# A hand-written issue order replaced by another: the backward chain of a recurrent attention layer

## The chip, the cores and the metric

The kernel runs on one core of one Trainium2 chip. The metric is the device time in microseconds (us) of one execution. The five engines are TensorE (PE, matrix products), VectorE (DVE), ScalarE (ACT), GpSimd (POOL) and SyncE (SP). Each runs its own instructions in the order in which they were issued, and waits on semaphores for the others. Here SP only issues DMAs; POOL issues DMAs too, and copies tiles.

## The reference

The reference is a forward pass and its gradients. `A` is attention with a recurrent memory over 64 segments, `B` a dense layer with a squared ReLU; both work on the same normed input.

```python
for s in range(n_seg):                       # 64 segments of 32 rows, 8 memory rows in front
    h = jnp.concatenate([mem, xs], axis=1)
    q, k, v = (jnp.einsum('btd,dhe->bhte', h, W) for W in (Wq, Wk, Wv))
    scores = jnp.where(mask, jnp.einsum('bhqe,bhke->bhqk', q, k) * scale, -1e9)
    o = jnp.einsum('bhqk,bhke->bhqe', softmax(scores), v)
    o = jnp.einsum('bhte,hed->btd', o, Wo)
    mem = o[:, :M, :]                        # the next segment's memory
    outs.append(o[:, M:, :])
...
_out, _vjp = jax.vjp(_f, A_x, A_mem0, A_Wq, A_Wk, A_Wv, A_Wo, B_w1, B_b1, B_w2, B_b2)
_grads = _vjp(grad_out)
```

The model width is 512; there are 32 heads of 128. The memory makes the segments a chain: forward from segment 0 to 63, and the gradients backward from 63 to 0. All outputs are bfloat16.

## The kernel before

The kernel has these stages: the norm and the dense layer; the forward chain; a pass over the "left" rows (the memory rows of four segments at a time, taken together); the backward chain, which is the one changed; and the products for the weight gradients.

**The backward chain.** One segment is a *step* (`bwd`, L1307), and four steps are a *block*. Steps run from segment 63 down, 64 in 16 blocks; "step 0" to "step 3" below are the places in a block in the order of time. A step on PE is, by the names in the order:

- `o0mm`, `o1mm`: two projections of the incoming gradient by Wo (L391), 16 matmuls each. `o0ev`, `o1ev` evict them (ACT); `o0fl`, `o1fl` transpose them, `o0te`, `o1te` (DVE) evict those. They read tile `GT`, in which the step before put its memory gradient (`Ha`, `Hb`); that is the chain.
- `vp0`, `vp1`: products for the gradient of v, with tiles `PD` and `PGD` (L1379, L1381); `vea`, `veb`, `vla`, `vlb` evict them (ACT).
- `s0`, `s1`: scores' gradients (L436), then four DVE operations each, `d10` to `d40` and `d11` to `d41` (L538 to L548), which give `gS`, and a transpose on DVE, `tu0`, `tu1` (L449).
- `kp0`, `kp1` and `qp0`, `qp1`: 32 short products each (L589) for the gradients of k and q. `kp` needs `gS` and `qN`; `qp` needs the transposed `gS`, `kN` and `kLs`. Evictions: `kea`, `keb`, `kla`, `klb`, `qea`, `qeb`, with a 0 or 1.
- `vg`, `kg`, `qg`, 0 and 1: six long products with the weights (L459), 16 matmuls of 512 columns each, all summed in one bank; the last one's second half goes to another bank.
- `ra`, `rb`: the sum's eviction; `ta`, `tb`: four transposes (L494); `Ha`, `Hb`: sums over head groups into the next step's `GT`; `xa`, `xb`: the other rows.

Pairs of products share PSUM tiles: `vp`, `kp0`+`qp0` and `kp1`+`qp1` take the same two tiles in turn, so each waits for the evictions of the one before.

**Left work**, once a block, for the block before (`left`, L1208): twelve products of eight matmuls, `L.G0` to `L.I3` (L1247), their sums `L.ra0` to `L.ra3`, `L.ta`, `L.tb`, `L.xt`; DMA transposes `L.vtr`, `L.ktr`, `L.qtr` into tile `gNat` (one buffer) and their stores `L.vst`, `L.kst`, `L.qst`; the stores of tiles `G4` (gv, gk, gq; one buffer for four steps) in halves, `L.vo0` to `L.ko1` (512 KB each); and `L.gs`, `L.gst`, `L.sl`, `L.sx`, `L.lq`, `L.gl`, `L.ldt`, `L.ldv`, `L.ldk`, which load the next block's tiles or store this one's.

**Loads of a step.** A load that is played at one step fetches for the next step (L1473). On POOL's queue: `ldp` (tile P, two buffers), `ldq` (qN), `ldn` (kN), with the copies `pb` (P into PD, four) and `vc` (two) between them on the same engine. On SP's queue: `ldk` (kLs, four DMAs of 16 KB) and `vtr` (a DMA transpose into `vl`). All but P have one buffer, so each waits until its tile's last reader is done.

**The order.** All of this is issued from a written list, `B_ORDER` (L1148): four strings, one after the other for each block. `play` (L623) reads them; each plus sign shifts an entry to a step (or, behind "L.", a block) one later. The list alone sets the order on every engine and in every queue: a waiting instruction holds up all that stands behind it on its engine. Which engine evicts what is set apart (`ENGS`), and stays.

Of the kernel before, what the change touches and what calls it, by code (L numbers as in the profile page):

```python
# [26 lines left out]
def kernel(  # L27
# [35 lines left out]
    L = M + SEG  # L63
# [119 lines left out]
    with sb("p1b", 2) as p1b, sb("p1", 1) as p1:  # L183
# [66 lines left out]
        for rb in range(NRB):  # L250
# [45 lines left out]
            xb = p1b.tile([P, RCB, D], BF16, name="xb", tag="xb", bufs=1)  # L296
# [322 lines left out]
    def on_engines(act, vec):  # L619

        return dict([(n, acp) for n in act.split()] + [(n, vcp) for n in vec.split()])
# [365 lines left out]
    with sb("la", 2) as la, sb("ls", 2) as ls, sb("lo", 1) as lo_, sb("wg", 2) as wg, psum("lpp", 1) as lpp, psum("lr", 4) as lr:  # L987
# [158 lines left out]


    B_ORDER = (  # L1148
# [6 lines left out]
        "tb++++ Ha++++ Hb++++",  # L1155
# [5 lines left out]
        "rb++++ ta++++ L.vtr+ ldp+++++ Ha++++ tb++++ Hb++++",  # L1161
# [5 lines left out]
        "tb++++ ldp+++++ Hb++++",  # L1167
        "o0mm++++ o1mm++++ L.ldt++ o0ev++++ ldq+++ ldn+++ vc+++ L.ra3+ xb+++ o1ev++++ xa+++ vtr++++ o0fl++++ "
# [4 lines left out]
        "L.I0++ ra++++ rb++++ ta++++ kla1++++ tb++++ L.H0++ Ha++++ Hb++++ L.ldk++")  # L1173
    ENGS = on_engines(
        "L.ra0 kea0 keb0 keb1 kla0 kla1 o0ev o1ev qea0 qea1 qeb0 ra vea veb vla vlb",
        "kea1 klb0 klb1 o0te o1te qeb1")
# [497 lines left out]
```

## Time and profile before

| | |
|---|---|
| median of three runs | 2915.46 us (2913.0 to 2922.69) |
| profiled execution | 2925.15 us, of which its span 2923.3 |
| PE busy | 2721.1 us, 93% of the span |
| backward chain | 1400.1 to 2345.8 us of the span, 945.7 us |
| DMA engines' busy share in it | 0.74 |
| mean granted clock of PE in it | 0.96 |

The profile is of one execution. Times in it are from the start of the span. "Busy" is the time in which an engine had an instruction under way; matmuls overlap. A line like "L459 PE MATMUL" names the source line, which can be that of a helper. The waits view names who ended an engine's idle time; the chain view follows the last instruction back to what released it at each step. "SPq" is a DMA being issued by SP; its time there is the issue, and the data land later.

### The profile page before, as it was taken

What the parts mean: (1) busy time and instruction counts of PE and PEld (TensorE: products, weight loads), DVE (VectorE), ACT (ScalarE), POOL (GpSimd) and SP (SyncE); (2) the same over time, 40 slices, a digit from 0 to 9 for tenths busy, and PEclk for the clock granted to TensorE, in tenths of its full rate; (3) what the DMA queues carried; (4) which work ended last, traced back from release to release, by engine and by line L of the source; (5) the groups of instructions that cost most, each with busy time, mean ns of one, the idle gap of its engine ahead of it and who ended that gap; (6) DMA issues with size and microseconds to landing.
All of it is one profiled execution on the core that took longest, in us unless ns stands there. A gap on an engine that the chain in (4) does not pass through costs nothing.

```text
span 2923.3 us, 116288 instructions
## 1 busy us (share of the span) xinstructions
PE 2721.1 (93%) x51700; PEld 1476.2 (50%) x51700; DVE 1297.6 (44%) x3790; ACT 1030.6 (35%) x2362; POOL 655.3 (22%) x1262
## 2 busy tenths in 40 slices
PE   7997899999999888889899999998999899999999
PEld 3453455555555555547445545554555444444444
DVE  5452466666666565444445544554455401100000
ACT  2332354444544444433333433433343301111111
POOL 0000100000000001122434343343333324332221
PEclk9998899999999999899899999999999999999999
DMA  9639367677776676999577777777777799999993
GB/s 249 214 101 292 94 166 191 178 193 184 181 196 171 166 170 167 230 260 259 145 181 176 175 197 202 177 183 201 189 172 184 215 280 226 222 211 234 205 206 79
DMA packets 796536, 564.17 MB, mean 193 GB/s; under 512 B 584593, under 2 KB 687138, under 8 KB 792706
## 3 DMA queue, kind: packets, MB, share of 16 engines
q1 hardware_dynamic: 753922, 424.58, 63.3%
q0 software_dynamic: 42112, 132.16, 14.4%
q8 instruction: 405, 6.64, 1.0%
q14 instruction: 97, 0.79, 0.1%
HBM read 191.51 MB, written 234.37 MB: 146 GB/s over the span
## 4 chain that ended last, share of the span: by engine, by line
PE 77%; DMA 11%; DVE 5%; SPq 3%; issue 3%; ACT 1%; POOL 0%; ACTq 0%; DVEq 0%; POOLq 0%
PE ps_gw L1635 17%; PE ps_proj L391 15%; PE ps_gR L459 11%; PE ps_R L459 5%; PE ps_L L349 3%; PE b_pp L589 3%; PE ps_tr L164 3%; PE ps_RL L1247 3%; DMA b_kLs<-S_NL 3%; PE ps_w L1102 2%; PE ps_sc L436 2%; PE f_pp L589 2%; PE b_T L494 1%; PE f_T L494 1%; PE ps_w L1097 1%
## 5 line engine op out<-in xcount | busy, mean ns | idle before, releaser
L1635 PE MATMUL ps_gw<-gn,HNc 128*128 128x512 bf16 x1920 | 416.8, 379 | 0.0
L1635 PEld LDWEIGHTS <-HNc 128*128 128x128 bf16 x1920 | 187.8, 98 | 223.6
L373 ACT CAST f_N<-ps_proj 128x512 bf16<-128x512 f32 x320 | 183.8, 580 | 202.5 <-PE ps_proj L391 200.9
L1568 ACT CAST wt<-ps_gw 128x512 bf16<-128x512 f32 x128 | 74.1, 587 | 450.6 <-PE ps_gw L1635 402.2
L391 PEld LDWEIGHTS <-X 128*32 128x32 bf16 x6144 | 154.3, 96 | 149.8 <-DVE X L503 21.4
L1551 DVE TENSOR_TENSOR gx<-ps_rows,gb 128x512 f32<-128x512 f32 x16 | 11.1, 692 | 426.6 <-PE ps_rows L1549 426.6
L891 POOL COPY kM<-f_kT 128x256 bf16<-128x256 bf16 x64 | 25.6, 400 | 739.9 <-DVE f_kT L376 565.9
L1635 PE MATMUL ps_gw<-GOc,gn 128*128 128x512 bf16 x640 | 141.6, 384 | 10.9 <-ACT wt L1568 9.4
L459 PE MATMUL ps_gR<-Wv,gv 128*32 128x512 bf16 x2048 | 145.9, 407 | 1.2 <-issue 1.2
L391 PE MATMUL ps_proj<-Wq,X 128*32 128x512 bf16 x2048 | 136.1, 382 | 7.2 <-DVE X L962 4.5
L459 PE MATMUL ps_gR<-Wk,gk 128*32 128x512 bf16 (+1 forms) x2048 | 141.1, 390 | 1.4 <-ACT gk L373 0.7
L373 ACT CAST gk<-b_pp 128x256 bf16<-128x256 f32 x192 | 70.7, 379 | 179.7 <-PE b_pp L589 116.0
L459 PE MATMUL ps_R<-Wo,OT 128*32 128x256 bf16 x4096 | 132.9, 286 | 1.1 <-DVE OT L376 1.1
L391 PE MATMUL ps_proj<-Wk,X 128*32 128x512 bf16 x2048 | 133.1, 384 | 0.7
L373 ACT CAST gON<-ps_proj 128x512 bf16<-128x512 f32 x128 | 74.9, 585 | 156.9 <-PE ps_proj L391 156.9
L391 PE MATMUL ps_proj<-Wv,X 128*32 128x512 bf16 x2048 | 129.9, 378 | 0.0
L391 PE MATMUL ps_proj<-Wo,GT 128*32 128x512 bf16 x2048 | 124.2, 384 | 4.2 <-DVE GT L1292 3.5
L1569 POOL DMA_DIRECT2D out_dram<-wt x120 | 64.8, 542 | 258.3 <-ACT wt L1568 243.5
L459 PE MATMUL ps_gR<-Wq,gq 128*32 128x512 bf16 (+1 forms) x2048 | 118.5, 343 | 0.9 <-issue 0.9
L1328 POOL COPY PD<-b_P 32x320 bf16<-32x320 bf16 x256 | 114.7, 448 | 8.0
L459 PEld LDWEIGHTS <-OT 128*32 128x32 bf16 x4096 | 108.1, 101 | 9.3 <-DVE OT L376 1.3
L1323 POOL DMA_DIRECT2D b_P<-S_A x63 | 33.8, 537 | 336.9 <-issue 103.5
(281 smaller groups left out, 5352.6 us busy)
## 6 DMA issues: line engine op xcount, KB each, us to landing
S_A<-f_N SPq DMA_DIRECT2D x64, 512.0 KB
out_dram<-wt POOLq DMA_DIRECT2D x134, 128.0 KB, 5.1
S_A<-f_N SPq DMA_DIRECT2D x64, 256.0 KB
S_GB<-gv SPq DMA_DIRECT2D x32, 512.0 KB
S_GB<-gq SPq DMA_DIRECT2D x32, 512.0 KB
S_GB<-gk SPq DMA_DIRECT2D x32, 512.0 KB
b_kN<-S_A POOLq DMA_DIRECT2D x63, 256.0 KB, 4.5
b_qN<-S_A POOLq DMA_DIRECT2D x63, 256.0 KB, 3.9
```

What stands on the lines that cost most here:

```text
L164: nc.tensor.transpose(ps_ap, in_ap, ident[base:base + k, base:base + k])
L349: nc.tensor.matmul(ps[:], lhsT=x(dc), rhs=Wqkv[t][:, dc, c0:c0 + 512], start=(dc == 0), stop=(dc == DC - 1))
L373: nc.scalar.copy(out, in_)
L391: nc.tensor.matmul(o, lhsT=hT[:, dc, :], rhs=x, start=(dc == 0), stop=(dc == DC - 1), tile_position=(0, 32 * g))
L436: nc.tensor.matmul(sc3[32 * g:32 * g + 32, k, c:c + n], lhsT=qT[:, 4 * h + k, g, :], rhs=kT[:, 4 * h + k, g, :], start=(mask is None), sto ...
L459: nc.tensor.matmul(R[32 * g:32 * g + 32, 0:(cs.stop - cs.start) * P].rearrange("p (a b) -> p a b", b=P), lhsT=XT(k, g), rhs=x[:, cs, :], s ...
L589: nc.tensor.matmul(o, lhsT=N_[32 * g:32 * g + m, kk * P:(kk + 1) * P], rhs=X(kk)[32 * g:32 * g + m], start=(i == 0), stop=(i == len(jobs) ...
L1247: nc.tensor.matmul(ps["R", i][32 * g:32 * g + 32, :].rearrange("p (a b) -> p a b", b=P), lhsT=B_[n][:, k, g, :], rhs=W(g * KH + k), start= ...
L1328: nc.gpsimd.tensor_copy(PD[32 * g:32 * g + 32, g], C["P"][32 * g:32 * g + 32, :, 0:L])
L1568: nc.scalar.copy(wt[:], ps[:])
L1569: eng(dst, wt[:])
L1635: nc.tensor.matmul(ps[:], lhsT=l(rc), rhs=r(rc), start=(n == 0), stop=(n == RC_ALL - 1))
```

## The change

`B_ORDER` is replaced by another list of the same 292 entries. Nothing else is changed: the same operations on the same engines, with the same tiles and buffers. The short products of a step, its evictions, loads and copies, and the left work stand at other places. The new strings are cut at other points than the old ones (a step begins inside a string), so the plus signs differ too.

```diff
     B_ORDER = (
-        "o0mm++++ pb+++ o1mm++++ L.vo1+ L.qst o0ev++++ L.vo0+ xa+++ L.xt L.qo0+ o1ev++++ o0fl++++ xb+++ L.ra0+ "
-        "vp0++++ o0te++++ L.G2+ vea++++ s0++++ d10++++ o1fl++++ d20++++ ldp++++ d30++++ ldq+++ vla++++ o1te++++ "
-        "vp1++++ ldn+++ ldp+++++ L.I1+ L.G1+ vlb++++ d40++++ veb++++ L.ko0+ s1++++ d11++++ L.ko1+ ldk+++ kp0++++ "
-        "vg1++++ tu0++++ L.qo1+ keb0++++ d21++++ qp0++++ kla0++++ vg0++++ kea0++++ d31++++ qeb0++++ d41++++ "
-        "kg0++++ klb0++++ vtr++++ tu1++++ qp1++++ ldn++++ L.sx+ qeb1++++ qea0++++ qg0++++ qea1++++ kp1++++ "
-        "qg1++++ keb1++++ kea1++++ kg1++++ vc++++ klb1++++ kla1++++ ra++++ pb++++ rb++++ ldq++++ L.H2+ ta++++ "
-        "tb++++ Ha++++ Hb++++",
-        "o0mm++++ o0ev++++ o1mm++++ o1ev++++ xb+++ o0fl++++ vp0++++ xa+++ o0te++++ vla++++ s0++++ o1fl++++ "
...
+        "Hb++ o0mm+++ o1mm+++ L.H3 L.lq+ xb++ o0ev+++ o0fl+++ o1ev+++ xa++ o0te+++ ldn++ vp0+++ vea+++ o1fl+++ "
+        "o1te+++ s0+++ vp1+++ s1+++ d10+++ d20+++ ldq++ d30+++ vg0+++ vlb+++ L.gl+ d40+++ kp0+++ vla+++ veb+++ tu0+++ "
+        "d11+++ qp0+++ keb0+++ d21+++ pb+++ d31+++ kla0+++ d41+++ qea0+++ vg1+++ klb0+++ kea0+++ L.vo1+ L.ra3 kg0+++ "
+        "L.ldv+ kp1+++ klb1+++ qeb0+++ tu1+++ L.qo0+ qg0+++ qp1+++ kea1+++ kla1+++ keb1+++ L.ldk+ kg1+++ qea1+++ "
+        "qeb1+++ qg1+++ ra+++ L.G0+ rb+++ ta+++ tb+++ Ha+++ Hb+++ o0mm++++ o1mm++++ L.ta L.ktr+",
+        "L.vo0+ xb++ o0ev+++ o0fl+++ vc++ o1ev+++ vp0+++ vea+++ L.qo1+ xa++ o0te+++ o1fl+++ L.ko0+ ldp+++ s0+++ "
+        "o1te+++ vtr+++ ldn++ vla+++ L.kst+ d10+++ ldk++ vp1+++ s1+++ d20+++ d30+++ d40+++ L.I0+ L.vtr+ vlb+++ L.H0+ "
+        "L.ko1+ ldq++ tu0+++ L.tb kp0+++ qp0+++ L.xt veb+++ keb0+++ kea0+++ L.gs+ ldq+++ d11+++ pb+++ d21+++ L.sx+ "
+        "qeb0+++ klb0+++ kla0+++ vg1+++ vg0+++ d31+++ qea0+++ kg0+++ d41+++ tu1+++ vc+++ qg0+++ qp1+++ kp1+++ L.vst+ "
+        "qea1+++ L.ra0+ qeb1+++ klb1+++ kea1+++ keb1+++ kla1+++ qg1+++ kg1+++ ra+++ ldn+++",
...
```

Read out for a block in the middle (the block of left work is the one before, `L.lq`, `L.gl`, `L.ldt`, `L.ldv`, `L.ldk` load for the next block; "now" marks a load for the step in which it is played, the others are for the next one), PE's products stand so:

```
step 0 before: o0mm o1mm o0fl vp0 G2 s0 o1fl vp1 I1 G1 s1 kp0 vg1 qp0 vg0 kg0 qp1 qg0 kp1 qg1 kg1 H2 ta tb
step 0 after:  o0mm o1mm L.ta o0fl vp0 o1fl s0 vp1 s1 I0 H0 L.tb kp0 qp0 vg1 vg0 kg0 qg0 qp1 kp1 qg1 kg1 I1 ta tb
step 1 before: o0mm o1mm o0fl vp0 s0 o1fl vp1 H1 s1 vg0 kp0 qp0 vg1 qg0 kp1 kg0 qp1 I2 kg1 qg1 G3 ta tb
step 1 after:  o0mm o1mm G1 o0fl vp0 o1fl s0 vp1 s1 vg0 kp0 qp0 vg1 qg0 kg0 kp1 qp1 kg1 qg1 H1 ta tb
step 2 before: o0mm o1mm o0fl vp0 s0 o1fl vp1 vg0 s1 kp0 vg1 qp0 I3 kg0 kp1 qp1 qg0 kg1 qg1 H3 ta tb
step 2 after:  o0mm o1mm G2 o0fl vp0 o1fl s0 vp1 s1 vg0 H2 kp0 qp0 vg1 kg0 I2 qg0 kp1 qp1 G3 kg1 qg1 I3 ta tb
step 3 before: o0mm o1mm o0fl vp0 o1fl s0 vp1 s1 vg0 kp0 L.tb qp0 vg1 kg0 kp1 G0 qp1 L.ta qg0 kg1 qg1 I0 ta tb H0
step 3 after:  o0mm o1mm H3 o0fl vp0 o1fl s0 vp1 s1 vg0 kp0 qp0 vg1 kg0 kp1 qg0 qp1 kg1 qg1 G0 ta tb
```

And the queues of SP and POOL:

```
SP before    step 0: vo1 qst vo0 qo0 ko0 ko1 ldk(now) qo1 vtr sx       step 1: ldk(now) ktr vtr vtr(step 3) kst ldk L.vtr
             step 2: sl vst gs gl gst                                  step 3: ldt vtr ldk(now) qtr lq
SP after     step 0: ktr vo0 qo1 ko0 vtr kst ldk(now) L.vtr ko1 gs sx vst ldk   step 1: qtr vtr gst
             step 2: sl ldk(now) vtr vtr(step 0) ldk ldt qst           step 3: lq gl vo1 qo0
POOL before  step 0: pb(now) ldp ldq(now) ldn(now) ldp(step 2) ldn vc pb ldq    step 1: ldp(step 3)
             step 2: ldq(now) vc(now) pb(now) ldn(now) ldp(step 0)     step 3: ldq(now) ldn(now) vc(now) pb(now) vc ldv L.ldk
POOL after   step 0: vc(now) ldp ldn(now) ldq(now) ldq pb vc ldn       step 1: ldp ldp(step 3) pb ldn vc
             step 2: ldq(now) ldp(step 0) pb vc                        step 3: ldn(now) ldq(now) pb ldv L.ldk
```

More of the change, by code (lines that the diff above doesn't have):

```diff
@@ L1148 @@
     B_ORDER = (
[6 rows of a table removed]
-        "tb++++ Ha++++ Hb++++",
[5 rows of a table removed]
-        "rb++++ ta++++ L.vtr+ ldp+++++ Ha++++ tb++++ Hb++++",
[5 rows of a table removed]
-        "tb++++ ldp+++++ Hb++++",
-        "o0mm++++ o1mm++++ L.ldt++ o0ev++++ ldq+++ ldn+++ vc+++ L.ra3+ xb+++ o1ev++++ xa+++ vtr++++ o0fl++++ "
[4 rows of a table removed]
-        "L.I0++ ra++++ rb++++ ta++++ kla1++++ tb++++ L.H0++ Ha++++ Hb++++ L.ldk++")
[4 rows of a table added]
+        "qeb1+++ qg1+++ ra+++ L.G0+ rb+++ ta+++ tb+++ Ha+++ Hb+++ o0mm++++ o1mm++++ L.ta L.ktr+",
[5 rows of a table added]
+        "rb++ L.I1+ ta++ ldk++ tb++ Ha++ Hb++ o0mm+++ L.qtr+ ldp+++ o1mm+++ o0ev+++ L.G1+ o0fl+++ o1ev+++ xb++ vp0+++ "
[3 rows of a table added]
+        "qea1+++ vc+++ klb1+++ kla1+++ qg1+++ L.H1+ ra+++ ta+++ rb+++ tb+++ Ha+++ Hb+++",
[4 rows of a table added]
+        "vc+++ L.I3+ vtr++++ kla1+++ ra+++ L.ra2+ rb+++ ldk+++ L.ldt++ L.qst+ ta+++ Ha+++ tb+++")
     ENGS = on_engines(
```

20 rows, old and new, of the table B_ORDER are left out of this document.

## The prediction

> **What bounds the kernel now.** I read the page first, then the stretches of the changed stage, then who ended TensorE's waits there, then one block on SP's queue and in the chain of waits.
>
> ```profile
> span 2923.3 us, 116288 instructions
> PE 2721.1 (93%) x51700; PEld 1476.2 (50%) x51700; DVE 1297.6 (44%) x3790; ACT 1030.6 (35%) x2362; POOL 655.3 (22%) x1262
> ```
>
> TensorE (PE) bounds the kernel, but its busy share hides short waits. The backward chain is the stretch 1400.1 to 2345.8 us. One block of it (four steps; step 3 is 1795.0, then step 0 of the next block and its steps 1 and 2) follows under it:
>
> ```profile
> core 0: us, PE busy (x) PEld busy (x) DVE busy (x) ACT busy (x) POOL busy (x), PEclk, DMA share, GB/s
> 1400.10:2345.80 945.70, 881.58 (x22878) 478.43 (x22879) 464.92 (x1454) 360.44 (x980) 365.62 (x708) 0.96 0.74 187
> 1795.00:1810.20 15.20, 13.82 (x365) 7.49 (x368) 7.50 (x24) 5.49 (x15) 8.64 (x17) 1.00 0.81 215
> 1810.20:1827.10 16.90, 15.64 (x372) 8.11 (x368) 6.93 (x24) 6.05 (x16) 4.32 (x9) 0.90 1.02 247
> 1827.10:1840.20 13.10, 12.93 (x357) 7.27 (x356) 7.92 (x23) 5.34 (x15) 5.21 (x11) 1.00 0.54 111
> 1840.20:1853.30 13.10, 12.68 (x350) 6.87 (x348) 6.33 (x21) 5.53 (x15) 4.60 (x9) 1.00 0.78 166
> ```
>
> All steps do nearly the same work, yet steps 3 and 0 take 15.2 and 16.9 us against 13.1. From the timeline's first `o0mm` matmuls the means are 16.6, 13.3, 13.0 and 15.5 us (steps 0 to 3), 58.4 a block. In step 0 the DMA engines are full (1.02) and the granted clock is 0.90. Who makes PE wait, and what SP issues just then:
>
> ```profile
> PE b_pp L589 <- DMA b_kLs<-S_NL: 12.8, 16, 3.2
> PE b_pp L589 <- DVE gS L548: 6.5, 9, 0.9
> PE b_pp L589 <- DMA b_qN<-S_A: 3.0, 4, 1.6
> ```
>
> ```profile
> 1802.79 0.37 SPq L1234 DMA_DIRECT2D S_GB<-gv  x1
> 1803.21 0.42 SPq L1279 DMA_DIRECT2D S_GL<-gNat  x1
> 1803.68 1.15 SPq L1234 DMA_DIRECT2D S_GB<-gv  x1
> 1804.92 0.57 SPq L1234 DMA_DIRECT2D S_GB<-gq  x1
> 1805.54 4.38 SPq L1234 DMA_DIRECT2D S_GB<-gk  x2
> 1809.96 4.78 SPq L608 DMA_DIRECT2D b_kLs<-S_NL  x4
> ```
>
> ```profile
> 1809.96 8.25 DMA b_kLs<-S_NL
> 1818.21 0.05 issue
> 1818.26 0.18 PE b_pp L589
> ```
>
> The last two fences are the mechanism. `qp0` of step 0 needs `kLs`, four loads of 16 KB on SP's queue. They are issued behind five 512 KB stores of G4, land at 1818.2, 15.5 us after the first store was issued and 23.3 us after step 3 began, and are on the chain. Over 14 blocks the product after `qp0` starts 24.3 us after step 3 began, and step 0 ends 7.6 us later: 31.9 for steps 3 and 0 together, 26.35 for steps 1 and 2.
>
> **The change, part by part.** No instruction is added or removed; both orders hold the same 4,672 entries. What moves:
>
> *Inside a step.* (a) `o1fl` now stands ahead of `s0`, so `vp0` and `o1fl` cover `o0te`. In steps 1 and 2 `s0` waits 0.19 us today; saved twice. (b) `qp0` follows `kp0` directly. `kp0` starts some 0.14 us after `d40` ends and its slot is 0.3; `tu0` takes 0.43 and 0.1 to be seen: 0.2 of waiting, in steps 1 and 3. Step 0 and step 2 have left products ahead of `kp0`, which hide it. `kp0` itself waits 0.2 to 0.25 for `d40` in steps 1 and 3 (0.18 today in step 2). (c) In step 0 only `kp1` (0.29) lies between `qp1` and `qg1`, in step 1 only `qp1` (0.30) between `kp1` and `kg1`; an eviction takes 0.37 and 0.25 to start and be seen: 0.33 lost each time. (d) left products: steps 1 and 2 get seven instead of five, at 0.45 to 0.5 each; step 3 gives three away, its rest lies ahead of a DMA wait. Laid end to end from slots of the trace (first matmul to first matmul of the next, unthrottled: two projections 1.84, six gathers 5.6, the small products 2.9, two sums 0.75; 11.15 a step), step 1 is 11.15 + 1.0 + 0.25 + 0.25 + 0.33 + 0.1 = 13.1, step 2 is 11.15 + 2.4 + 0.2 = 13.75. Checked on today's step 2: 11.15 + 1.0 + 0.9 of waits = 13.05, seen 13.03. Steps 1 and 2 together: 26.85, 0.5 more than now. Between none of their waits (25.9) and twice them (27.9) I take the laid-out value.
>
> *Queues.* This is the larger part. SP's order around step 0 becomes `vo1`, `qo0` (now in step 3), `ktr`, `vo0`, `qo1`, `ko0`, `vtr`, `kst`, and only then step 0's `ldk`. Ahead of `ldk` there were `vo1`, `qst`, `vo0`, `qo0`, `ko0`, `ko1`. So five stores of 512 KB stand ahead of it as before, but also two DMA transposes, and a store (`kst`) that waits for one of them to land; everything behind `kst` in SP's queue (`ldk`, `L.vtr`, `ko1`, `gs`, `sx`, `vst`) waits with it, and PE waits for `ldk`.
>
> Prices from the trace's packet list in this stage, as time of all 16 DMA engines: 142,743 packets of 256 bytes hold them 258 us, nine transposes a block in 16 blocks: 1.79 us each. 33,805 packets of 1 KB, 101 us: a gq or gk half (512) 1.53. 4,096 of 4 KB on SP's queue, 42 us: a gv half (128) 1.3. 12,288 of 2 KB, 78 us: an S_GL store (128) 0.81. 13,971 of 4 KB on POOL's queue, 183 us: a 256 KB load (64) 0.84. Work ahead of `ldk` on SP's queue: before 2 x 1.3 + 0.81 + 3 x 1.53 = 8.0; after 2 x 1.3 + 3 x 1.53 + 2 x 1.79 + 0.81 = 11.6. POOL's loads beside it (PGD, gOL, GL, qNL, P, qN, kN) are the same 4.65.
>
> When does it start? `vo1` waits for `veb` of step 3: `vp1` ends at 3.93 (1.84 of projections, H3 0.44, the flips, `vp0` and `s0`), then vlb, vla and veb follow on ScalarE at 3.8, 4.0 and 4.2, veb takes 0.59, so `vo1` goes out 4.95 us into step 3, against 7.8 in the block shown. `qo0` waits for `qeb0` (`qp0` ends at 6.1, five evictions 0.3 apart: 7.4), `ktr` for `kla1` and `klb1` after `kp1` (8.8), `qo1` for `qea1`, `qeb1` after `qp1` (10.6); `vtr` for POOL's `vc` at 11.05 (`pb` from 4.0, five `ldv` issues to 8.5, two `ldk` to 9.6, two copies of 1.45). DMA engines busy from 6.5, 0.6 idle between, 16.25 of work: 23.3. The other way: 4.95 + 15.5 as seen + 3.6 more = 24.0. I take 23.6 for `kLs`; bounds 21 (the half us idle gone and a fifth of the packets faster) and 25.5.
>
> PE's own order would want it sooner: step 3 is 11.15 + 1.0 (H3, G0) + 0.25 + 0.25 + 0.1 = 12.75, and `qp0` stands 5.65 into step 0 (1.84 + sums of the block before 0.37 + 0.43, flips, `vp`, `s` 1.75, I0 and H0 0.95, `kp0` 0.3): 18.4 in all. So PE waits about 5 us there, and the 0.2 waits of step 3 and the slow `d40` (next) vanish in it. After it come 0.3 + 7.7 (`vg1`, `vg0`, `kg0`, `qg0`, `qp1`, `kp1`, `qg1`, `kg1`, I1, `ta`, `tb` = 0.98 + 0.88 + 0.88 + 0.98 + 0.3 + 0.29 + 0.33 + 0.87 + 0.87 + 0.95 + 0.37) and the clock. The trace's clock record has 13 half-speed stretches in the stage after its first 20 us, 51 us together, all in steps 0 and 3: 25.6 lost, 1.6 a block. One 3.41 us stretch a block costs 1.7; between 0.5 and 3.4 I take that, as the wait is longer than most now.
>
> The row on the clock: step 0 above has 0.90, though its longest PE gap is 0.86 us. The Trainium skill (TensorE: Matmul & The Clock Gate, "HAM oscillation — how this bites in real kernels") puts the limit at idle gaps of about 3.4 us. By that rule a wait under 3.4, `kLs` before 21.8, would cost no clock, and the sum there would be 25 us lower than by the row; this trace speaks against it.
>
> *DVE and POOL.* `pb` (four copies of 0.45) now lies at 4.0 to 5.95 of step 3, over `d40`. Today `vc` lies there, and `gS` L548 takes 0.97 instead of 0.32 in half the blocks. Nothing or 0.65, hidden behind `kLs` either way. POOL's other loads go out 1 to 2 us earlier against step 0 and cost nothing while `kLs` is last.
>
> *Sum.* Steps 3 and 0: 23.6 + 0.3 + 7.7 + 1.7 = 33.3 against 31.9, at 15 passages: +21. Steps 1 and 2: +0.5 x 16 = +8. Together +29. The profiled execution was 2925.15 (span 2923.3 and 1.85 around it), 9.7 above the median of the runs; the sum would make it 2954, and on the median 2915.5 + 29 = 2944.
>
> **Rivals.**
> A, faster: the ring is not backed up, because the stores start 2.9 us earlier and are spread. `kLs` lands at 19, PE hardly waits, half the clock loss goes: 19 + 0.3 + 7.7 + 0.5 = 27.5, 4.4 less at 15 passages, -66 + 8: 2858. It decides from `kLs` before 21.7 (31.9 - 0.5 - 9.7). For it: the stage's DMA share is 0.74, and steps 1 and 2 have room. Against: 1.02 in step 0, and `kLs` issues that take 4.78 us for four. Chance 0.22.
> B, slower still: `ko1` now waits behind `L.vtr`, which waits for `kst` to land; it lands near 29, while `keb1` of step 0, which overwrites what it reads, wants 28.4 to 30. ACT waits up to 1.1, PE with it, and a second half-clock stretch follows (1.7): 2.8 x 15 = 42 on the forecast: 2986. Chance 0.14.
> C, no change: the two waits balance, or the order does not do what its words say because PE's queue order hardly matters behind the same DMA bytes: 2915. Chance 0.12.
>
> **The numbers.** The forecast has 0.52. Slower by over 0.3% (9 us, about what a measurement of this kernel tells from none) are it and B: 0.66; faster A: 0.22; the same 0.12. The low end, 2892, is `kLs` at 20.1; the high end, 2987, takes in B and `kLs` at 25.5 (+1.9 x 15 = 28).
>
> **What would show it.** Right: in step 0 a PE gap of 4 to 6 us inside `qp0`, ended by `kLs`; SP's `kst` issued after a wait for `gNat`; steps 1 and 2 at 13.1 and 13.8; a half-clock stretch in most step 0s; `s0` without a wait. Wrong: steps 3 and 0 together under 31, or `kLs` landing before `qp0` is due; or the time lost in steps 1 and 2, in waits between `kp1` and the gathers, which I have priced by rows of other neighbours.

## The result and the profile after

The changed kernel takes 3034.64 us (median of four runs, 3026.39 to 3043.02) against 2918.08 of the kernel before beside it: a ratio of 1.041 [1.037, 1.045], 117 us slower. The forecast was 2944, +29. The direction was right; the size was not: 3035 lies above the high end of the range, 2987. The profiled execution took 3026.43, with a span of 3024.6.

The page of the kernel after first:

```profile
span 3024.6 us, 116331 instructions
PE 2732.1 (90%) x51700; PEld 1486.3 (49%) x51700; DVE 1300.3 (43%) x3790; ACT 1023.8 (34%) x2362; POOL 656.4 (22%) x1262
```

PE has 11 us more of busy time in a span that is 101 us longer: most of the time went into waits, not into work. The stretches of the backward chain, and of one block in it (step 3, then step 0 of the next block, its steps 1 and 2):

```profile
core 0: us, PE busy (x) PEld busy (x) DVE busy (x) ACT busy (x) POOL busy (x), PEclk, DMA share, GB/s
1386.24:2448.83 1062.59, 901.99 (x22878) 494.51 (x22879) 468.59 (x1455) 354.13 (x980) 366.96 (x709) 0.94 0.67 167
1832.04:1846.10 14.06, 12.86 (x350) 6.89 (x350) 7.31 (x22) 5.34 (x15) 8.25 (x16) 1.00 0.92 243
1846.10:1867.12 21.02, 15.70 (x361) 8.89 (x360) 7.39 (x25) 5.74 (x16) 3.15 (x6) 0.84 0.84 226
1867.12:1881.28 14.16, 12.73 (x349) 7.00 (x348) 6.72 (x21) 5.34 (x15) 6.52 (x14) 1.00 0.67 118
1881.28:1896.63 15.35, 13.78 (x373) 7.66 (x372) 7.92 (x23) 5.54 (x15) 4.73 (x9) 1.00 0.31 67
```

The stage is 1062.6 us instead of 945.7, 117 more, which is all of the loss (the execution profiled before had spent 14 us more ahead of the stage, so the spans differ by less). Step 0 takes 21.0 us, of which PE is busy 15.7, at a granted clock of 0.84. The DMA engines are less busy over all of step 0 than before (0.84 against 1.02), as the step is longer; up to the point for which PE waits they are nearly full, as shown below. Who ends PE's waits in the stage, and ACT's for a store:

```profile
PE b_pp L589 <- DMA b_kLs<-S_NL: 49.4, 20, 4.6
ACT gv L373 <- DMA S_GB<-gv: 39.1, 13, 4.8
PE b_pp L589 <- DVE gk L376: 18.6, 32, 0.6
PE b_pp L589 <- ACT b_gkL L373: 14.9, 16, 0.9
PE b_pp L589 <- ACT b_gvL L373: 14.3, 10, 2.8
```

Two families are seen. `kLs` makes PE wait four times as long as before, and `vea` (ACT writes gv) now waits for `vo0` to land, and `kp0` of step 0 with it (the line of `b_gvL`: `kp0` takes the PSUM tile that `vea` and `vla` evict). The lines of `gk` and `b_gkL` came to under 1 us each before: they are now 48 waits inside the steps for evictions, 0.58 and 0.93 us each in the mean. SP's queue in the block shown:

```profile
1837.02 0.34 SPq L1229 DMA_DIRECT2D S_GB<-gv  x1
1839.55 0.54 SPq L1229 DMA_DIRECT2D S_GB<-gq  x1
1842.76 1.27 SPq L1265 DMA_TRANSPOSE gNat<-b_gkL  x1
1844.08 0.57 SPq L1229 DMA_DIRECT2D S_GB<-gv  x1
1844.76 0.56 SPq L1229 DMA_DIRECT2D S_GB<-gq  x1
1845.37 1.68 SPq L1229 DMA_DIRECT2D S_GB<-gk  x1
1847.14 5.04 SPq L1331 DMA_TRANSPOSE b_vl<-S_A  x1
1852.27 0.53 SPq L1274 DMA_DIRECT2D S_GL<-gNat  x1
1852.89 2.30 SPq L608 DMA_DIRECT2D b_kLs<-S_NL  x4
```

The order is the one that the prediction read from the list: `vo1`, `qo0`, `ktr`, `vo0`, `qo1`, `ko0`, `vtr`, `kst`, `ldk`. From step 3's start (1832.04) `vo1` goes out at 4.98 and `qo0` at 7.51 (4.95 and 7.4 were forecast), but `ktr` at 10.7 instead of 8.8 (11.4 in the mean), and the issue of `vtr` alone holds SP for 5.04 us. `kst` goes out 0.09 us after it, here and in each of the 15 passages from a step 3 to a step 0: it does not wait for the tile that `ktr` fills, as the prediction had it. The chain of waits runs through it to PE:

```profile
1852.89 0.32 SPq L608
1853.21 0.06 issue
1853.27 3.62 DMA b_kLs<-S_NL
1856.89 0.05 issue
1856.94 0.77 PE b_pp L589 x19
```

`kLs` lands at 1856.89, 24.85 us after step 3 began; the product behind `qp0` starts at 25.6 in this block and at 26.5 in the mean. From the issue of `vo1` to this landing, in the block shown of the kernel before and then in this one (columns as above):

```profile
1802.79:1818.21 15.42, 13.36 (x338) 7.18 (x326) 6.76 (x24) 4.99 (x13) 5.24 (x12) 1.00 0.97 332
1837.02:1856.89 19.87, 13.94 (x385) 7.72 (x381) 9.21 (x30) 5.25 (x15) 7.37 (x14) 0.93 0.94 253
```

The DMA engines are nearly full in both, 0.97 and 0.94. That is 15.0 us of transfers before and 18.7 after: `kLs` is late because its place in the queue has more transfers ahead of it, not because the engines stand idle.

### The profile page after: what moved, and what is told of

The parts are those of the page before. It is cut to its first block, busy times and chain, and to the rows that moved or that the text cites. A ratio compares the mean times of both kernels' runs of the same rounds, so it can differ in the third digit from the quotient of the medians.

```text
span 3024.6 us, 116331 instructions
## 1 busy us (share of the span) xinstructions
PE 2732.1 (90%) x51700; PEld 1486.3 (49%) x51700; DVE 1300.3 (43%) x3790; ACT 1023.8 (34%) x2362; POOL 656.4 (22%) x1262
## 3 DMA queue, kind: packets, MB, share of 16 engines
q0 software_dynamic: 42112, 132.16, 14.6%
## 4 chain that ended last, share of the span: by engine, by line
PE 74%; DMA 9%; SPq 5%; DVE 5%; ACT 4%; issue 3%; POOL 0%; ACTq 0%; DVEq 0%; POOLq 0%
PE ps_gw L1630 16%; PE ps_proj L391 14%; PE ps_gR L459 11%; PE ps_R L459 4%; PE b_pp L589 3%; PE ps_L L349 3%; PE ps_tr L164 3%; SPq L1331 2%; DMA b_kLs<-S_NL 2%; PE ps_RL L1242 2%; PE ps_w L1102 2%; PE ps_sc L436 2%; PE f_pp L589 1%; PE f_T L494 1%; ACT gk L373 1%
## 5 line engine op out<-in xcount | busy, mean ns | idle before, releaser
L391 PEld LDWEIGHTS <-X 128*32 128x32 bf16 x6144 | 152.3, 96 | 149.6 <-DVE X L503 21.6
L891 POOL COPY kM<-f_kT 128x256 bf16<-128x256 bf16 x64 | 25.6, 400 | 733.9 <-DVE f_kT L376 559.9
L459 PE MATMUL ps_gR<-Wk,gk 128*32 128x512 bf16 (+1 forms) x2048 | 157.3, 389 | 20.9 <-DVE gk L376 8.9
L459 PE MATMUL ps_gR<-Wv,gv 128*32 128x512 bf16 x2048 | 156.7, 438 | 1.7 <-issue 1.7
L459 PE MATMUL ps_gR<-Wq,gq 128*32 128x512 bf16 (+1 forms) x2048 | 128.3, 348 | 10.9 <-ACT gq L373 8.7
L459 PEld LDWEIGHTS <-gk 128*32 128x32 bf16 x2304 | 66.5, 101 | 93.4 <-ACT gk L373 34.5
L459 PEld LDWEIGHTS <-gq 128*32 128x32 bf16 x2816 | 86.8, 99 | 52.0 <-ACT gq L373 19.3
```

Of the source, the lines that this page charges most:

```text
L391: nc.tensor.matmul(o, lhsT=hT[:, dc, :], rhs=x, start=(dc == 0), stop=(dc == DC - 1), tile_position=(0, 32 * g))
L459: nc.tensor.matmul(R[32 * g:32 * g + 32, 0:(cs.stop - cs.start) * P].rearrange("p (a b) -> p a b", b=P), lhsT=XT(k, g), rhs=x[:, cs, :], s ...
```

## The experiments

All are edits of the list alone. Every kernel does all of the work. Step lengths are means over the blocks, from the first `o0mm` matmul of a step to that of the next. The "clock" column is the time that a block loses to half-speed stretches (half of their length).

| kernel | ratio to before | steps 3+0 | steps 1+2 | clock |
|---|---|---|---|---|
| before | 1 | 32.1 | 26.4 | 2.0 |
| after | 1.041 [1.037, 1.045] | 36.2 | 29.5 | 4.0 |
| e1_ldk_first | 1.035 [1.031, 1.038] | 35.5 | 29.3 | 2.6 |
| e2_evictions | 1.025 [1.022, 1.028] | 35.6 | 27.0 | 4.2 |
| e3_both | 1.021 [1.018, 1.024] | 35.9 | 26.5 | 3.6 |
| e7_stores_first | 1.007 [1.004, 1.009] | 31.7 | 27.9 | 2.2 |
| e7b_stores_without_evictions | 1.018 [1.014, 1.021] | 31.9 | 30.4 | 1.8 |
| e9_sx_early | 1.003 [1.001, 1.006] | 32.4 | 27.1 | 2.3 |
| e11_after_repaired | 1.007 [1.004, 1.010] | 32.4 | 27.1 | 2.3 |
| e4_before_transposes_first | 1.024 [1.019, 1.028] | 36.8 | 26.0 | 4.2 |
| e5_before_kea1_first | 1.001 [0.998, 1.003] | 32.3 | 26.4 | 1.6 |
| e6_before_ldk | 1.002 [1.000, 1.005] | 32.6 | 26.2 | 2.2 |
| e8_before_stores_early | 1.012 [1.009, 1.016] | 32.4 | 26.2 | 1.6 |
| e10_before_stores_early_2 | 1.012 [1.009, 1.015] | 33.6 | 25.9 | 2.4 |

**e1_ldk_first: is the place of `ldk` the loss?**

```diff
 step 3, SP's queue
-  vo1 qo0 | ktr vo0 qo1 ko0 vtr kst ldk(step 0) L.vtr ko1
+  vo1 qo0 ldk(step 0) | ktr vo0 qo1 ko0 vtr kst L.vtr ko1
```

> The changed kernel with one entry moved: the load of kLs for step 0 is played in step 3, directly behind qp1 (its buffer's last reader), so in SP's queue it stands ahead of ktr, vo0, qo1, ko0, vtr and kst instead of behind them. PE's order is the same. Queue theory (kLs is late because of what stands ahead of it on SP's queue, and the half clock in step 0 follows from that wait): the 2.5 us inside qp0 of step 0 go, and about half of the 3.4 us that the clock costs there; 15 passages, some 65 us less, near 2968. Rival (the same bytes must pass whatever the order, so another transfer takes its place, first of all vo0, whose landing vea waits for, or qN): under 20 us less, above 3010. Rival (the short waits between products carry all of the loss): no change, 3034.

Measured: 3020.1 us, 0.6% of before less than after (the two intervals touch), as the first rival had it: under 20 us. The wait for `kLs` is gone, and others stand in its place, over the whole stage:

```profile
ACT gk L373 <- DMA S_GB<-gk: 64.2, 30, 4.2
ACT gv L373 <- DMA S_GB<-gv: 42.6, 12, 6.5
DVE gk L376 <- DMA S_GB<-gk: 41.2, 15, 4.5
PE b_pp L589 <- ACT b_gvL L373: 28.1, 14, 4.6
```

`kea` and `keb` of step 0 write tiles that `ko0` and `ko1` still read, `vea` one that `vo0` reads; G4 has one buffer. PE's wait behind `vea` doubles, from 14.3 to 28.1 us. `kLs` was only the last of several transfers that are late together. So the forecast's single term (`kLs` late) was too simple, and its rival B (`ko1` late) was waiting behind it, to show as soon as the first is removed. What fell is the clock's loss, from 4.0 to 2.6 us a block.

**e2_evictions: the waits inside the steps.**

```diff
 order of products and evictions in the list (excerpt)
-step 1: kg0 kp1 kea1 qp1 keb1          step 2: keb0 kea0 kla0 qp0 ... qg0 kp1 tu1 kea1 qp1
+step 1: kp1 kea1 keb1 kg0 qp1          step 2: qp0 keb0 kea0 kla0 ... kp1 tu1 kea1 keb1 qg0 qp1
-step 3: qg0 qp1 kea1 kla1 keb1         step 0: qg0 qp1 kp1 qea1 qeb1
+step 3: kea1 kla1 keb1 qg0 qp1         step 0: qp1 qea1 qeb1 qg0 kp1
```

> The changed kernel with the evictions and the second short products at other places of a step, the queues as they are: in step 3 kea1, kla1, keb1 ahead of qg0 and qp1; in step 0 qp1, qea1, qeb1 ahead of qg0; in step 1 kp1, kea1, keb1 ahead of kg0; in step 2 qp0 ahead of keb0, kea0, kla0, and kp1, tu1, kea1, keb1 ahead of qg0. Tile theory (an eviction listed between two products that share a PSUM tile makes the second product wait for it, and one listed behind the second product waits for that): the slots kp1 to qp1 (0.65 in steps 1 and 2), kp0 to qp0 of step 2 (0.91), qp1 to kg1 of step 3 (0.8), kp1 to qg1 of step 0 (0.7) fall to 0.1 to 0.3; 1.1 us in step 1 and 1.4 in step 2 for 16 blocks, and about 1.5 in steps 3 and 0 together, since kla1 lets ktr out 1.9 us earlier: 55 to 65 us less, near 2975. Rival (kLs alone): steps 1 and 2 gain at most the 10 us of my old sum, above 3020.

Measured: 2989.4 us, 1.6% of before less than after. Step 2 falls from 15.31 to 13.44, step 1 from 14.15 to 13.51. PE's waits in the stage, for the same evictions as above:

```profile
PE b_pp L589 <- DMA b_kLs<-S_NL: 59.9, 22, 5.3
PE b_pp L589 <- ACT b_gkL L373: 5.0, 13, 0.4
```

The wait for ACT's `gkL` is a third of what it was, DVE's `gk` has left the list, and `kLs` has grown by 10 us. **e3_both** has both edits.

> Both edits in the changed kernel: the load of kLs for step 0 behind qp1 of step 3, and the evictions and short products moved. If the two causes are all and independent: 3034 less 65 and less 55, near 2915, what the kernel before takes. If they share a cause (a full ring whatever the order): near 2960. Below 2900 only if the clock loss in step 0 goes entirely.

Measured: 2981.1 us. Steps 1 and 2 are at 26.5, as before the change; steps 3 and 0 still take 35.9, since the stores stand as in e1: in the stage ACT waits 52.9 us to write gv until `S_GB<-gv` has landed, and 70.1 to write gk. What is left is in SP's queue.

**e7_stores_first and e7b: the stores of G4 ahead of the transposes.**

```diff
 SP's queue (e7: e3 and this; e7b: e1 and this)
-  vo1 qo0 ldk(step 0) | ktr vo0 qo1 ko0 vtr kst L.vtr ko1 gs sx vst
+  vo1 vo0 qo0 ldk(step 0) qo1 ko0 ko1 | ktr vtr kst L.vtr gs sx vst
```

> The changed order with step 0's ldk behind qp1 of step 3 and the short products moved ahead of their long ones (as in e3_both), and now also all six stores of G4 ahead of the DMA transposes: vo1 and vo0 directly behind veb of step 3, qo1, ko0 and ko1 behind qeb1; then ktr, vtr, kst. Theory (step 0 waits for whichever of kLs and the G4 stores stands last behind ktr, vtr and kst): the waits ahead of kp0 (1.97 us a block, vea waits for vo0) and ahead of kg1 (1.96, keb1 and kea1 wait for ko1) go down to some 0.2 each, and about 2 of the 3.28 us of clock with them: 5.5 x 15 = 83 us off 2981, so 2890 to 2905, under the kernel before. Rival (the DMA engines are full in step 0, so that any order only moves the wait): the wait shows up behind another load or store, and the time stays at 2960 to 2985.

> The stores and ldk as in e7, with the short products where the changed kernel has them. Theory: step 0 is repaired as in e7, steps 1 and 2 stay as slow as after the change (13.9 and 15.3 us): 2940 to 2955, some 45 us above e7. Rival (full DMA engines): 3005 to 3020, as e1_ldk_first.

Measured: 2940.5 and 2977.6 us. The theory's mechanism holds, its size was too hopeful: steps 3 and 0 fall by 4.1 us (e3 to e7) and by 3.6 (e1 to e7b), to where they were before the change, and the clock goes back with them. The waits for `S_GB` that were 176 us on ACT and DVE in e3 are one line of 10.6 us. SP's queue of e7, in the same place of a block:

```profile
1794.98 1.82 SPq L1229 DMA_DIRECT2D S_GB<-gv  x2
1797.51 0.55 SPq L1229 DMA_DIRECT2D S_GB<-gq  x1
1801.27 1.34 SPq L608 DMA_DIRECT2D b_kLs<-S_NL  x4
1802.72 0.54 SPq L1229 DMA_DIRECT2D S_GB<-gq  x1
1803.30 2.38 SPq L1229 DMA_DIRECT2D S_GB<-gk  x2
1805.73 3.80 SPq L1265 DMA_TRANSPOSE gNat<-b_gkL  x1
1809.63 1.86 SPq L1331 DMA_TRANSPOSE b_vl<-S_A  x1
```

The same transfers take the same queue; only what PE waits for has passed the transposes. e7 and e7b differ by 1.1% of before; alone the evictions brought 1.6% (e2), and beside the earlier `ldk` 1.3% (e1 to e3). So the two parts nearly add up.

**e9_sx_early.** In e7 step 1 has a new wait, seen in its waits view: `xb` writes tile XT, which `sx` has not yet stored, and `sx` stands behind `kst` and two transposes.

```profile
DVE b_XT L503 <- DMA S_XG<-b_XT: 31.8, 13, 4.1
PE b_pp L1374 <- DVE b_XT L503: 12.9, 10, 2.5
```

```diff
 SP's queue, step 0
-  kst L.vtr gs sx vst
+  kst sx L.vtr gs vst
```

> e7 with L.vtr and L.gs moved behind L.sx in SP's queue in step 0. In e7, vp0 of step 1 waits 0.93 us a block for xb, xb waits for the clearing of XT on POOL, and that waits for the store sx, which stands behind kst's wait, L.vtr and L.gs in SP's queue. Theory: sx goes out 2 to 5 us earlier and that wait goes: 0.8 to 1.1 us a block with its clock, 12 to 18 us off e7: 2920 to 2930, level with before. Rival (sx waits for kst in any case): 2935 to 2945, as e7.

Measured: 2929.1 us, 0.3% above before; step 1 falls from 14.3 to 13.4, as the theory has it, while in the one profiled execution step 0 gives 0.6 of it back. The same thing happens a third time: a store behind transposes that PE waits for at two removes.

**e4_before_transposes_first: the same cause put into the kernel before.** Only `ktr`, step 0's `vtr` and `kst` move ahead of step 0's `ldk`; all of PE's order stays.

```diff
 SP's queue of the kernel before, step 0
-  ko0 ko1 ldk(now) qo1 vtr sx ... ktr kst
+  ko0 ko1 ktr vtr kst ldk(now) qo1 sx ...
```

> The kernel before with only ktr, step 0's vtr and kst moved ahead of step 0's ldk in SP's queue, behind ko1. Theory (SP's queue serves in order, and kst waits for a transpose to land): kLs lands 3.5 to 5 us later, PE waits that long in qp0 of step 0, and a half-clock stretch goes with it: 4 to 6.3 us a block, 2980 to 3015. Rival (the place in the queue matters little because the same bytes are moved): within 0.3% of before.

Measured: 2991.3 us, +69. In SP's timeline `kLs` now goes out 11.2 us after `ktr`:

```profile
1825.34 4.41 SPq L1270 DMA_TRANSPOSE gNat<-b_gkL  x1
1829.84 3.67 SPq L1336 DMA_TRANSPOSE b_vl<-S_A  x1
1836.18 0.34 SPq L1279 DMA_DIRECT2D S_GL<-gNat  x1
1836.57 1.34 SPq L608 DMA_DIRECT2D b_kLs<-S_NL  x4
```

Here `kst` does wait, 6.43 us from the end of `ktr`'s issue. Not all of the 11.2 us is the price of the three entries: in the block shown of the kernel before, the issue of the four `kLs` loads itself took 4.78 us right behind the five stores, and here it takes 1.34. From the issue of `vo1` to PE's first product with `kLs` the mean went from 15.8 to 20.4 us, 4.7 more, where the prediction's prices for two transposes and `kst` give 4.4 (2 x 1.79 + 0.81). PE's waits for `kLs` in the stage go from 12.8 to 59.0 us and the clock's loss from 2.0 to 4.2 us a block. Three entries of 292, none of them on PE, cost 2.4%, as much as the queue's repair brings back in the changed kernel (2.3%, from after to e7b).

**e5_before_kea1_first: is the short wait made by the list alone?** The kernel before, with `kea1` listed ahead of `qp1` in step 2. `kea1` runs on DVE and `qp1` on PE, so no engine's own order changes; only the waits between them do.

> The kernel before with kea1 listed ahead of qp1 instead of behind it in step 2. Every engine keeps the order of its instructions; only the waits differ. Theory (products of k and q of one half share a PSUM tile, so that a product listed behind an eviction waits for it): the time from kp1's slot to qp1's rises by 0.5 to 0.7 us in each step 2, 16 times: 5 to 11 us, 0.2 to 0.4%. Rival (kea1 and qp1 touch other parts of the tile, and no wait is put between them): no wait in the trace, same time.

Measured in the timeline of PE and DVE: `kp1`, then `kea1`, then `qp1`, which waits for it.

```profile
1841.90 0.17 PE L589 MATMUL b_pp<-b_GL,b_qNL 32*128 32x16 bf16 x4
1842.20 0.42 DVE L376 CAST gk<-b_pp 128x256 bf16<-128x256 f32 x1 [1.39 <-PE b_pp L589]
1842.68 0.20 PE L589 MATMUL b_pp<-gST,b_kN 32*128 32x32 bf16 x4 [0.61 <-DVE gk L376]
```

In the kernel before `qp1` starts 0.22 us after `kp1` in the same block; here 0.97. In 15 of 16 blocks it is 0.97, where 14 of 16 had 0.21 or 0.22 before. `kp1` and `qp1` write different columns of the same tile (`qp` begins behind the 4 x 40 columns of `kp`). The wait is put between them because the list names a reader of that tile between its two writers. That the list alone makes the wait is shown (two tiles instead of one were not tried); in the time (1.0005 [0.998, 1.003]) it can't be told from none, as the step lost only 0.24 us net: `qp1` and `qg0` behind it take 0.31 and 0.88 in the mean, where they took 0.47 and 1.12.

**e6_before_ldk: does the kernel before gain by an earlier `kLs`?**

```diff
-  vo1 qst vo0 qo0 ko0 ko1 ldk(now)
+  vo1 qst vo0 ldk(now) qo0 ko0 ko1
```

> The kernel before with one entry moved: the load of kLs for step 0 stands behind vo0 in SP's queue instead of behind ko1, so two stores less (qo0, ko0, ko1 follow it). PE's order and every other entry are the same. Queue theory: the waits for kLs in step 0 (0.7 us in qp0 on the mean, more in single blocks) and some of the half clock go: 1.2 to 2 us a block, 18 to 30 us less, near 2893. Rival (the same bytes must pass, qN and P take its place): within 8 us of before.

Measured: 2927.5, no change. The waits for `kLs` halve (12.8 to 5.5 us) and `ACT gk <- S_GB<-gk` grows from 14.1 to 32.6. So in the kernel before, too, an earlier `kLs` alone only passes the wait on to the stores.

**e8, e10, e11: is there a faster order?** e8 puts all stores of G4 and step 0's `ldk` into step 3 of the kernel before.

```diff
 SP's queue of the kernel before (e8)
-step 3: vtr ldk(now) qtr lq                          step 0: vo1 qst vo0 qo0 ko0 ko1 ldk(now) qo1
+step 3: vtr ldk(now) vo1 vo0 ldk(step 0) qtr lq qo0 ko0 qo1 ko1    step 0: qst
```

> The kernel before with only SP's stores of G4 and one load earlier: vo1 and vo0 directly behind veb of step 3, step 0's ldk behind qp1 of step 3, then qo0, ko0, qo1 and ko1 behind qea1 of step 3 (they were spread over the first half of step 0). Theory (in the kernel before too, step 0 waits for what stands last in SP's queue): of step 0's 2.3 us of waits some 1.2 go (qp0 to vg0 0.68, s1 to kp0 0.3, part of vg1 to qp0) and about 1 of 1.56 of clock: 2.2 x 15 = 33 us, 2885 to 2900, 0.7 to 1.3% under before. Rival (the DMA engines are full in steps 3 and 0, so the earlier stores delay the loads of step 3 and of POOL's queue): step 0 gains, step 3 loses as much, within 0.3%.

Measured: 2949.4 us, slower. `lq` loads the tile that `qtr` reads, so it waits for the transpose to land, and four stores wait with it:

```profile
1797.00 1.25 SPq L1270 DMA_TRANSPOSE gNat<-b_gqL  x1
1801.57 0.35 SPq L1212 DMA_DIRECT2D b_gqL<-S_GQL  x1
1802.02 0.56 SPq L1234 DMA_DIRECT2D S_GB<-gq  x1
1802.63 0.64 SPq L1234 DMA_DIRECT2D S_GB<-gk  x1
```

Step 3 gains 0.6 and step 0 loses 0.8, where `kea0` waits for `ko0` (53.2 us over the stage). The other 34 us lie in the last block, where the left work waits for `lq`, and the next stage's loads are already under way. e10 moves `qtr` ahead and `lq` ahead of the four stores.

```diff
-  vtr ldk(now) vo1 vo0 ldk(step 0) qtr lq qo0 ko0 qo1 ko1
+  vtr qtr ldk(now) vo1 vo0 ldk(step 0) lq qo0 ko0 qo1 ko1
```

> e8 with two more entries of SP's queue moved: the transpose L.qtr directly behind step 3's vtr, and the load L.lq, which waits for that transpose to land, behind step 0's ldk and ahead of the four stores qo0, ko0, qo1, ko1. In e8 L.lq was issued 4.6 us after L.qtr and held the four stores back, and kea0 of step 0 waited for ko0 to land (53 us over 14 blocks); at the end of the stage the pair cost 34 us. Theory (the place behind a transpose is what costs, not the bytes): ko0 is issued some 4 us earlier, kea0's wait goes to under 1 us a block, step 0 falls from 17.45 to about 15, and the end of the stage is as before: 2880 to 2900. Rival (the DMA engines are full there): steps 3 and 0 stay at 32.1 together and only the 34 us at the end go: 2910 to 2920.

Measured: 2949.4 us. Step 0 falls to 16.5 (15 was expected), but step 3 rises to 17.1, because `qtr` now stands ahead of step 3's own `ldk` (`PE <- kLs` 21.6 us, 11 times); and the last block still loses 27 us, now with `gNat` waiting for its store. Both accounts missed this.

e11 removes e9's short waits in steps 3 and 1.

```diff
 the list of e9, step 3 (excerpt); in step 1, qeb0 qea0 ahead of keb0
-  qp0 keb0 kla0 qea0 vg1 klb0 kea0 kg0 kp1 klb1 qeb0 tu1 kea1 kla1 keb1 qg0 qp1 ldk kg1
+  qp0 keb0 kea0 kla0 qea0 vg1 klb0 qeb0 kp1 tu1 kg0 qp1 ldk kea1 keb1 qg0 klb1 kla1 kg1
```

> e9 with more entries moved inside steps 3 and 1: in step 3 kea0 directly behind keb0, qeb0 ahead of kp1, qp1 behind kg0 and ahead of kea1, keb1, kla1, klb1 in the list; in step 1 qeb0 and qea0 ahead of keb0. Theory (waits come from evictions listed between products of the same half): in step 3 vg1 to kg0 0.53, qg0 to qp1 0.50 and qp1 to kg1 0.39 go, in step 1 vg1 to qg0 0.36: 1.4 to 1.7 us a block, 22 to 27 us off e9, 0.2 to 0.6% faster than the kernel before. Rival (qp1 then waits for tu1, and kg1 for evictions that now wait for qp1): the waits move inside the step, and the time is that of e9, 0.3% slower than before.

Measured: 2933.3 us, no better than e9. Step 3 gets 0.6 shorter and step 0 0.6 longer: PE arrives earlier at step 0 and waits there for `qN` (28.4 us, 14 times), a load on POOL's queue. No order tried beats the kernel before. In eight of the orders, the kernel before among them, steps 3 and 0 take 31.7 to 32.6 together; in three blocks each of e7 and e11 the DMA engines were busy 0.80 to 0.97 of such a stretch. A floor set by the bytes moved fits that, but it was not tried by leaving bytes out, and stays open.

## Why the prediction was half right

**Right: the place, and that SP's queue makes the larger part.** It said that the loss would sit in step 0 inside `qp0`, ended by `kLs`, because two transposes and `kst` now stand ahead of `ldk`. The order in SP's queue, the issue of `vo1` and `qo0`, a half-clock stretch in most step 0s and `s0` without a wait are all in the trace; e4 shows that these three entries alone cost the kernel before 69 us.

Two parts of this came out otherwise. `kst` did not wait for a tile in the changed kernel; what held SP there was the issue of `vtr`, 4.8 us in the mean (3.5 to 7.2). And the PE gap, forecast at 4 to 6 us inside `qp0`, is 3.1 there (49.4 us over 16 blocks), with 1.3 ahead of it in `kp0`, behind the evictions that `vo0` makes late (14.3 and 6.0 us). That the sum, 4.4, lies in the forecast is luck: `kLs` came later than forecast, and so did PE, which reached `qp0` 22.1 us after step 3 began instead of 18.4.

**Wrong: its size, 33.3 against 36.2 for steps 3 and 0** (+44 us over 15 passages).

- *The landing of `kLs`, put at 23.6.* This is the term that failed. PE's first product with `kLs` starts at 25.5 in the mean and the product after `qp0` at 26.5, where 23.9 was forecast: 2.6 of the 2.9 us. The sum had the DMA engines start on 16.25 us of transfers at 6.5. From there to that product they are busy 0.95 of 19.0 us in the mean: 18.1 us of transfers. The two transposes are most of the difference: in that stretch their packets of 256 bytes hold the engines 5.0 us, 38 ns each, where the mean of the kernel before, 29 ns, gave 3.6. The price was taken from the whole stage, and it was used for its busiest part. `ktr` was also taken to go out by its own data (`kla1`, `klb1` after `kp1`, 8.8); but `kla1` stands behind `kea1` and `qp1` in the list and came at 10.5 in the block shown. That cost little, as the engines stood idle for 0.9 us where 0.6 was forecast.
- *What else is late.* Stores were counted as bytes ahead of `kLs`, not as things that PE waits for, and the clock, taken at 1.7 us a block in step 0, lost 3.4. In the changed kernel this adds little, as 1.5 of the 3.4 and the wait of `kp0` lie ahead of the landing of `kLs`, which hides them; behind it the clock lost 1.9. But it is why e1 gained so little.

**Wrong: steps 1 and 2, 26.85 against 29.5** (+42 us over 16 blocks). The step that failed is a term that the sums of steps 1 and 2 leave at nothing: a product that is listed behind an eviction of the PSUM tile that it shares waits for that eviction. The waits of point (c), 0.33 each, are others, those of a long product for its own data. An eviction listed between `kp` and `qp` of the same half costs 0.64 to 0.9 us; the new list has one such place in step 1 and two in step 2, 2.2 us a block. With it the laid-out 13.1 and 13.75 become 13.7 and 15.3, and the medians are 13.8 and 15.3; the rest of the 42 us is in three blocks whose step 1 took 14.6 to 16.7. With the evictions moved (e3) the same two steps take 26.5, so the laid-out slots were right for what they held. The prediction had named such waits as what would make it wrong ("waits between `kp1` and the gathers, which I have priced by rows of other neighbours"), but left them out of the range.

The two errors, 44 and 42, are nearly all of the 88 us between forecast and result.

**The rivals.** A (faster) never came near: its condition was `kLs` before 21.7. B (`ko1` late) is real but hidden behind `kLs` in the changed kernel; e1 and e3 bring it out, at 2.3 and 2.0 us of PE's time a block ahead of `kg1`, without the clock, where 1.1 was given. C was out by 117 us.

**The clock.** Step 0 of the block shown ran at 0.84, and PE's longest single wait in it is 2.9 us (`kLs`), behind one of 1.4. The Trainium skill (TensorE: Matmul & The Clock Gate, "HAM oscillation — how this bites in real kernels") ties the half clock to idle gaps over about 3.4 us. As in the kernel before, this trace loses clock with shorter gaps: in the block shown the half speed begins at 1854.0 us, 0.3 us into the wait for `kLs`, and the stretch that begins at 1478.6 us has a single wait of 1.03 us ahead of it.

## What to carry to other kernels

When an order is changed, walk each DMA queue for everything that an engine will wait for, loads *and* the stores that free a single buffer, and put those ahead of transposes and of any entry that itself waits for a transfer to land. If several are late together, removing the latest gains little (0.6% here, against 2.3% for all of them): count all that are late. And in a list from which waits are derived, keep the products that share a tile next to each other, with the evictions behind both, or with a long product between.

## What the runs showed of the hardware

- An issue on SP takes longer when much stands ahead in its queue: a transpose 1.25 us (`ktr` in the kernel before), 3.5 to 7.7 behind stores of 512 KB (`vtr` after the change, and `ktr` in e4 in all passages but one). The time of the issue is not shown to be a price of the transpose: four `kLs` loads took 4.78 us behind such stores, and one store of gk 7.63 in the last block of e8.
- An entry that waits for a transpose to land goes out 3.3 us after the end of its issue (`lq` in e8), 3.5 to 6.4 with another transpose between (`kst` in e4). The Trainium skill (DMA: Bandwidth & Descriptors, "Two DMAs through the same engine are not ordered") says that descriptors in one queue of one DMA engine start in order; e4 agrees, as three entries ahead of four loads of 16 KB cost 69 us.
- The half-speed stretches of the stage come in lengths of 3.41, 6.83, 10.24 and 17.07 us: 11 of 14 are of 3.41 before, 12 of 22 of 6.83 after (68 and 130 us in all).
